# X^T of batches 2 to 7 by DMA transposes instead of TensorE transposes, with one more slot before the first use

## The chip, the cores and the metric

The kernel runs on one core of a Trainium2 chip. The metric is the device time of one execution in microseconds (us). Some executions are slower whatever the kernel; a run counts as slow here when it is over 1.5% above the fastest of the same kernel. Ratios and intervals use fast runs alone.

## The reference

Causal block attention over 8 batches, 8 heads, 576 positions and 64 dimensions per head, followed by a gated feed-forward block (FFN) with an RMS norm in front. Cut to what matters:

```python
scores = where(block_i >= block_j, (q @ k.T) / sqrt(64), -1e9)     # blocks of 64
x   = (softmax(scores) @ v)            # to [4608 tokens, 512]
xn  = x / sqrt(mean(x*x) + 1e-6) * rms_g
g   = xn @ w_gate                      # 512 -> 1536
out = (g * sigmoid(g) * (xn @ w_val)) @ w_out
```

The FFN needs `xn` transposed (d_model on the partitions); this is the X^T of the title.

## The kernel before

The kernel is a software pipeline of slots. A slot holds the attention of one pair of heads (four slots per batch) with pieces of FFN work from a queue placed between the parts of the attention. The FFN works on chunks of 512 tokens (the first two have 256). A chunk first runs 12 pairs of a gate and a value piece (four TensorE matmuls of 512 columns each), and then four rows of a down projection (twelve matmuls each). I call these its gate/value phase and its down phase. In the queue's units a chunk is 144, of which the first 96 are the gate/value phase.

Matmul results land in buffers of PSUM; a buffer can be taken for the next result once the one in it has been read for the last time. A plain copy out of PSUM is called an eviction here. The parts that the change touches (cuts are marked with `# ...`):

```python
def norm_scale(b, tiles):
    XN = xn_tiles[b]
    XS = xs.tile([P, n, DM], BF16, name="XS")
    # ... root(): 1/sqrt of the mean square, 13 small VectorE operations
    def one(j, t):
        rs = norm_tiles[b, tiles[0], "rs"]
        nc.vector.tensor_scalar(out=XS[:, j, :], in0=XN[:, t, :],
                                scalar1=rs[:, j:j + 1], scalar2=None, op0=ALU.mult)
    return [root] + [lambda j=j, t=t: one(j, t) for j, t in enumerate(tiles)]

def norm_transpose(b, tiles, p):          # p: one of four groups of 128 columns
    x = pf.tile([P, 2 * BANK], BF16, name="fps")           # PSUM
    for j in range(len(tiles)):
        pe(nc.tensor.transpose(x[:, j * P:(j + 1) * P], XS[:, j, p * P:(p + 1) * P], ident))
    # ... for each chunk touched: ScalarE copies x to XT, times gscale (rms_g)

def up_gate(i, m):
    pg = pf.tile([P, BANK], FP32, name="fps")              # pf: four PSUM buffers
    # ... four matmuls into pg; ScalarE: th = tanh(pg / 2); VectorE: th = (th + 1) * pg
def up_val(i, m):
    pv = pf.tile([P, BANK], FP32, name="fps")
    # ... four matmuls into pv; VectorE: HT = th * pv

def down(i, s, part):
    # ... twelve matmuls into one PSUM buffer po, in three parts
    if part == 2:
        ob = obuf.tile([P, DM], FP32, name="ob")           # obuf: two buffers
        nc.scalar.mul(out=ob, in_=po, mul=0.5)
        sp(nc.sync.dma_start(out=out[r0:r0 + P, :], in_=ob))   # SyncE's queue, kept in order

def ffn(cost):
    # ... while the budget lasts: the next piece of the queue, and after it
    #     one waiting piece of norm work: if aside: aside.pop(0)()
```

and the order of events for a batch (s0 is the slot after its last attention pair), with the end of each slot:

```python
    at(norms, s0, norm_squares)            # ScalarE
    at(norms, s0 + 1, norm_scale)          # VectorE
    s1 = s0 + 2
    at(norms, s1, xt_by_pe)                # TensorE transposes, ScalarE evictions
    at(rels, s1, release)                  # the chunk enters the queue at this slot's end
    ready.append(s1 + 1)
    # ... at the end of every slot, what the FFN pieces have not taken is run at once:
    for f in todo + aside + rels.pop(s, []) + pp + loads.pop(s, []):
        f()
```

The norm pieces of a slot start halfway through it. SyncE's queue carries three things in one order: the attention's own DMA transposes (QKT from QKN, 128x1920), the output stores, and, after the change, the new transposes.

The softmax here doesn't subtract the row's maximum and nothing guards it: scores larger than these inputs give would overflow.

## Time and profile before

| | before |
|---|---|
| time, median of the first three runs | 416.3 us (415.96 to 418.01) |
| TensorE busy | 376.6 us, 90% |
| VectorE, ScalarE busy | 61%, 59% |
| chain of waits | 74% TensorE, 11% ScalarE, 9% VectorE |
| TensorE transposes of XS | 160 |

The groups that the change touches (line, engine, operation, out<-in, shapes, count | busy us, mean ns of one | idle before, releaser), from the view that keeps shapes apart:

```profile
L342 DVE TENSOR_SCALAR XS<-XN,y 128x512 bf16<-128x512 f32 x40 | 20.2, 546 | 0.2
L355 PE MATMUL fps<-ident,XS 128*128 128x128 bf16 x160 | 14.9, 220 | 2.6 <-DVE XS L342 2.6
```

What VectorE does in the first of these stretches, in order of time (start us, length us):

```profile
135.95 0.49 DVE L342 TENSOR_SCALAR XS<-XN,y 128x512 bf16<-128x512 f32 x1
136.35 0.68 DVE L391 SCALAR_TENSOR_TENSOR th<-th,fps 128x512 f32<-128x512 f32 x1
136.95 0.64 DVE L342 TENSOR_SCALAR XS<-XN,y 128x512 bf16<-128x512 f32 x1
137.51 0.67 DVE L403 TENSOR_TENSOR HT<-th,fps 128x512 bf16<-128x512 f32 x1
138.10 1.40 DVE L342 TENSOR_SCALAR XS<-XN,y 128x512 bf16<-128x512 f32 x3
```

The last of the chunk's gate and value results (`th`, `HT`) stand among the first two scalings. The other three come after them, in the down phase, where VectorE has little to do (2.22 us busy from 140 to 150 us). TensorE waited for VectorE's `th` or `HT` for only 0.4 us in the whole span:

```profile
PE st L89 <- ACT PT_95 L260: 6.9, 7, 1.6
...
PE st L89 <- ACT PT_96 L260: 4.2, 6, 1.6
...
PE fps L89 <- DVE HT L403: 0.2, 1, 0.2
PE fps L89 <- DVE th L391: 0.2, 1, 0.2
```

(That view lists who waited for whom: us in total, times, longest.)

### The profile page before, as it was taken

What the parts mean: (1) busy time and instruction counts of PE and PEld (TensorE: products, weight loads), DVE (VectorE), ACT (ScalarE), POOL (GpSimd) and SP (SyncE); (2) the same over time, 40 slices, a digit from 0 to 9 for tenths busy, and PEclk for the clock granted to TensorE, in tenths of its full rate; (3) what the DMA queues carried; (4) which work ended last, traced back from release to release, by engine and by line L of the source; (5) the groups of instructions that cost most, each with busy time, mean ns of one, the idle gap of its engine ahead of it and who ended that gap; (6) DMA issues with size and microseconds to landing.
All of it is one profiled execution on the core that took longest, in us unless ns stands there. A gap on an engine that the chain in (4) does not pass through costs nothing.

```text
span 416.1 us, 7914 instructions
## 1 busy us (share of the span) xinstructions
PE 376.6 (90%) x2952; PEld 211.5 (51%) x3000; DVE 254.3 (61%) x698; ACT 245.6 (59%) x490; POOL 143.3 (34%) x200
## 2 busy tenths in 40 slices
PE   1367887988999999999999999999999999999996
PEld 0235764666555555555555555555555545444442
DVE  3554976669468546864785478447845881761760
ACT  2367877786767566756676667666765526322321
POOL 5532899987625903670349042000000000000000
PEclk9999999999999999999999999999999999999999
DMA  8999999999949975995699579342211002002002
GB/s 198 171 244 239 175 78 104 153 171 144 169 61 121 166 119 66 125 176 100 74 109 171 112 75 114 90 99 57 38 52 52 2 26 76 2 0 101 2 0 101
DMA packets 156277, 42.98 MB, mean 103 GB/s; under 512 B 142928, under 2 KB 151632, under 8 KB 156240
## 3 DMA queue, kind: packets, MB, share of 16 engines
q0 software_dynamic: 100512, 16.53, 54.0%
q1 hardware_dynamic: 55728, 25.96, 29.1%
q8 instruction: 23, 0.38, 0.4%
q14 instruction: 14, 0.11, 0.1%
HBM read 37.75 MB, written 9.44 MB: 113 GB/s over the span
## 4 chain that ended last, share of the span: by engine, by line
PE 74%; ACT 11%; DVE 9%; DMA 4%; issue 2%; SPq 0%; ACTq 0%; DVEq 0%
PE fps L89 57%; PE st L89 9%; PE X L89 6%; DMA HT<-in_k_dram 4%; ACT PT_95 L260 3%; ACT sq L327 2%; DVE th L391 2%; DVE HT L403 2%; ACT PT_96 L260 2%; PE fps L355 2%; ACT XT L362 2%; DVE XS L342 1%; ACT th L390 1%; DVE QKT L181 1%; DVE XN L294 1%
## 5 line engine op out<-in xcount | busy, mean ns | idle before, releaser
L89 PE MATMUL fps<-XT,WG 128*128 128x512 bf16 (+1 forms) x466 | 112.0, 357 | 1.2 <-DVE th L391 0.2
L89 PE MATMUL fps<-XT,WV 128*128 128x512 bf16 (+1 forms) x467 | 111.3, 357 | 0.5
L390 ACT ACTIVATE th<-fps 128x512 f32<-128x512 f32 (+1 forms) x120 | 66.8, 556 | 69.2 <-PE fps L89 66.4
L391 DVE SCALAR_TENSOR_TENSOR th<-th,fps 128x512 f32<-128x512 f32 (+1 forms) x120 | 75.8, 632 | 44.7 <-ACT th L390 44.1
L89 PE MATMUL fps<-WO,HT 128*128 128x512 bf16 x412 | 101.7, 379 | 1.2 <-DVE HT L403 0.2
L403 DVE TENSOR_TENSOR HT<-th,fps 128x512 bf16<-128x512 f32 (+1 forms) x120 | 75.9, 633 | 8.9 <-DVE th L391 0.5
L89 PEld LDWEIGHTS <-WG 128*128 128x128 bf16 x480 | 43.3, 98 | 38.6 <-issue 0.7
L89 PEld LDWEIGHTS <-WV 128*128 128x128 bf16 x480 | 43.5, 98 | 38.0
L260 ACT ACTIVATE PT_95<-st 128x512 bf16<-128x512 f32 (+3 forms) x70 | 51.0, 759 | 19.1 <-PE st L89 18.9
L89 PEld LDWEIGHTS <-HT 128*128 128x128 bf16 x432 | 38.8, 98 | 39.3 <-DVE HT L403 0.7
L260 ACT ACTIVATE PT_96<-st 128x1024 bf16<-128x1024 f32 (+3 forms) x67 | 51.0, 786 | 5.2 <-PE st L89 4.9
L417 ACT ACTIVATE ob<-fps 128x512 f32<-128x512 f32 x36 | 21.6, 599 | 51.8 <-PE fps L89 36.9
L89 PE MATMUL st<-QKT 128*128 128x320 bf16 (+3 forms) x240 | 43.1, 294 | 2.5 <-ACT PT_96 L260 1.2
L89 PEld LDWEIGHTS <-QKT 128*128 128x128 bf16 x288 | 27.0, 98 | 26.1 <-issue 3.0
L80 POOL DMA_DIRECT2D VN_94<-in_v_dram x20 | 17.0, 865 | 48.5 <-PE X L89 35.3
L294 DVE TENSOR_TENSOR XN<-X,rd 128x320 f32<-128x320 f32 (+2 forms) x72 | 32.4, 453 | 1.7
L362 ACT ACTIVATE XT<-fps,gscale 128x256 bf16<-128x256 bf16 (+6 forms) x68 | 28.8, 501 | 3.4 <-PE fps L355 3.3
L80 POOL DMA_DIRECT2D VN_93<-in_v_dram x20 | 18.5, 959 | 31.0 <-PE X L89 30.6
L267 DVE MEMSET PT_96<- 64x64 uint32 (+2 forms) x64 | 6.9, 112 | 35.8 <-ACT PT_96 L260 32.8
L80 POOL DMA_DIRECT2D QKN_92<-in_k_dram x30 | 22.9, 762 | 10.7 <-issue 9.9
L327 ACT ACTIVATE sq<-XN 128x512 bf16<-128x512 f32 x40 | 25.3, 633 | 0.1
L80 POOL DMA_DIRECT2D QKN_91<-in_k_dram x30 | 22.7, 757 | 5.3 <-issue 3.4
(82 smaller groups left out, 334.5 us busy)
## 6 DMA issues: line engine op xcount, KB each, us to landing
out_dram<-ob SPq DMA_DIRECT2D x36, 256.0 KB, 2.0
VN_93<-in_v_dram POOLq DMA_DIRECT2D x16, 128.0 KB, 5.6
VN_94<-in_v_dram POOLq DMA_DIRECT2D x16, 128.0 KB, 6.4
WG<-in_moe_w_gate_dram POOLq DMA_DIRECT2D x4, 384.0 KB, 13.7
WV<-in_moe_w_val_dram POOLq DMA_DIRECT2D x4, 384.0 KB, 16.5
WO<-in_moe_w_out_dram POOLq DMA_DIRECT2D x2, 768.0 KB, 25.7
QKN_91<-in_k_dram POOLq DMA_DIRECT2D x24, 64.0 KB, 4.0
QKN_91<-in_q_dram POOLq DMA_DIRECT2D x24, 64.0 KB, 3.8
```

What stands on the lines that cost most here:

```text
L80: return chain("POOL", nc.gpsimd.dma_start(**kw))
L89: pe(nc.tensor.matmul(dst, w, r, start=start, stop=stop))
L260: nc.scalar.activation(out=self.PT[:, n * T4 + a:n * T4 + e], in_=st[:, a:e], func=AF.Exp, scale=SM_SCALE)
L267: nc.vector.memset(blk[:, :, 0:BLK], 0.0)
L294: nc.vector.tensor_tensor(out=xn_tiles[self.b][:, t0:t0 + n, hd * D:(hd + 1) * D], in0=xv[:, :, 0:D], in1=rd.to_broadcast([P, n, D]), op=A ...
L327: nc.scalar.activation(out=sq, in_=XN[:, t, :], func=AF.Square, accum_out=ss[:, j:j + 1])
L355: pe(nc.tensor.transpose(x[:, j * P:(j + 1) * P], XS[:, j, p * P:(p + 1) * P], ident))
L362: nc.scalar.activation(out=xt_tiles[i][:, p, lo - a:hi - a], in_=x[:, lo - g0:hi - g0], func=AF.Copy, scale=gscale[:, p:p + 1])
L390: nc.scalar.activation(out=th[:, 0:n], in_=pg[:, 0:n], func=AF.Tanh, scale=0.5)
L391: nc.vector.scalar_tensor_tensor(out=th[:, 0:n], in0=th[:, 0:n], scalar=1.0, in1=pg[:, 0:n], op0=ALU.add, op1=ALU.mult)
L403: nc.vector.tensor_tensor(out=ht_tiles[i][:, m, :], in0=th[:, 0:n], in1=pv[:, 0:n], op=ALU.mult)
L417: nc.scalar.mul(out=ob, in_=po, mul=0.5)
```

## The change

The intent is to take the transposes of XS off the busiest engine. For batches 2 to 7 the XS tile is transposed by DMA from SyncE's queue straight into XT. The ScalarE copy that applied rms_g goes with the TensorE transposes, so the scaling takes rms_g, broadcast over the partitions in GB, as a second operand. The chunk's release is put one slot later, so that the transposes have time to land.

```diff
+    GB = const.tile([P, DM], FP32, name="GB")
@@ norm_scale
         def one(j, t):
             rs = norm_tiles[b, tiles[0], "rs"]
-            nc.vector.tensor_scalar(out=XS[:, j, :], in0=XN[:, t, :],
-                                    scalar1=rs[:, j:j + 1], scalar2=None, op0=ALU.mult)
+            if b >= 2:
+                nc.vector.scalar_tensor_tensor(out=XS[:, j, :], in0=XN[:, t, :],
+                                               scalar=rs[:, j:j + 1], in1=GB,
+                                               op0=ALU.mult, op1=ALU.mult)
+                turn(b, t, XS[:, j, :])
+            else:
+                # ... as before
+
+    def turn(b, t, src):
+        # ... for each chunk that the tile touches:
+                sp(nc.sync.dma_start_transpose(out=xt_tiles[i][:, :, lo - a:hi - a],
+                                               in_=src[lo - g0:hi - g0, :]))
@@ start
+    nc.sync.dma_start(out=GB, in_=moe_rms_g.partition_broadcast(P))
@@ order of events
-        at(norms, s1, lambda b=b, tiles=tiles: xt_by_pe(b, tiles))
+        if not b >= 2:
+            at(norms, s1, lambda b=b, tiles=tiles: xt_by_pe(b, tiles))
+        else:
+            s1 += 2 - 1
```

More of the change, by code (lines that the diff above doesn't have):

```diff
@@ L341, in one @@
             rs = norm_tiles[b, tiles[0], "rs"]
-            nc.vector.tensor_scalar(out=XS[:, j, :], in0=XN[:, t, :],
-                                    scalar1=rs[:, j:j + 1], scalar2=None, op0=ALU.mult)
-        return [root] + [lambda j=j, t=t: one(j, t) for j, t in enumerate(tiles)]
+            if b >= 2:
[4 more added lines that the diff above has]
+            else:
+                nc.vector.tensor_scalar(out=XS[:, j, :], in0=XN[:, t, :],
+                                        scalar1=rs[:, j:j + 1], scalar2=None, op0=ALU.mult)
+        return [root] + [lambda j=j, t=t: one(j, t) for j, t in enumerate(tiles)]
+    def turn(b, t, src):
+        g0 = b * S + t * P
+        g1 = min(g0 + P, (b + 1) * S)
+        for i, (a, e) in enumerate(chunks):
+            lo, hi = max(a, g0), min(e, g1)
+            if lo < hi:
+                if i not in xt_tiles:
+                    xt_tiles[i] = xtp.tile([P, HP, e - a], BF16, name="XT")
+                sp(nc.sync.dma_start_transpose(out=xt_tiles[i][:, :, lo - a:hi - a],
+                                               in_=src[lo - g0:hi - g0, :]))
     bounds = [0, 256] + list(range(512, NT + 1, 512))
```

## The prediction

> **What bounds the kernel.** TensorE. In stretches of 10 us, TensorE is 97 to 100% busy from 110 us to 410 us; the chain of waits is 74% TensorE. Busy time hides small gaps, so I summed issue spacings from the timeline: a feed-forward (FFN) matmul of 512 columns takes 0.2155 us (four in 0.862 us), the attention of one head pair about 2.26 us, a group of five TensorE transposes 0.28 us (142.23 to 142.51 us). From 108 us to the end that is 1164 x 0.2155 + 21 x 2.26 + 24 x 0.28 = 305 us for 303.5 us of time. No hidden stall is left to recover; time falls only by TensorE work removed after 108 us. Before 108 us TensorE is 70 to 90% busy.
>
> **What the change removes.** 120 of the 160 transposes, in 24 groups, all after 108 us: 24 x 0.28 = 6.7 us of TensorE, all on the critical path. Also 48 of the 68 ScalarE evictions into X^T (about 0.5 us each) and 24 PSUM tiles; off the path. The page's 14.9 us of transpose busy time (11.2 us for 120) overstates it: neighbours overlap part.
>
> **What it adds.** 30 VectorE scalings with a second operand instead of a plain scalar: 0.48 us each now, estimated 0.55 to 0.69 us (this operation reading PSUM takes 0.686 us). At most 6 us on an engine 61% busy: off the path. 33 DMA transposes of up to 128x512 on SyncE's queue. The existing transposes, 3.75 times larger, hold the queue for 1.4 to 3.6 us and land 4.1 to 9.4 us (median 5.1) after issue; scaled, about 0.5 us of issue each. The Trainium skill's "DMA: Bandwidth & Descriptors" (Latency and other measured facts) gives 261 GB/s effective with a non-contiguous middle dimension; this trace's transposes with their fixed time come to less than 100 GB/s, and I use the trace. The last piece is issued about the end of its slot; the first use comes a full slot (about 9.8 us) plus the 12-unit reserve (2.6 us) later, so it should land in time. The scale row adds 256 KB at the start, when DMA is full: 0 to 1 us.
>
> **What it moves.** FFN chunks of batches 2 on are released one slot later. Steady slots keep their FFN share, but slots 11 to 15 spread one chunk's 132 units over five slots instead of four: 26 units, about 8 us instead of 9.8 us per slot. In the thinner slots before (83 to 97 us) TensorE lost 0.3 to 0.9 us at a time to exponentials queued behind squares. I expect 0 to 1.5 us lost there, mostly in slot 12, which has the squares. The displaced work runs later, where TensorE is dense.
>
> **Sum.** -6.7, +0.7 (thin slots), +0.4 (start): 416.3 - 5.6 = 410.7 us. Range 408.8 to 413.5. Faster by over 2% (below 408.0) 0.07, within 2% 0.89, slower 0.04.
>
> **What would show it.** TensorE transposes 40 instead of 160, X^T evictions 20; TensorE busy about 11 us less; still 98% or more from 150 us to the end; no TensorE wait on a DMA transpose; small new waits on exponentials between 108 and 150 us; first dense moment within 1 us of before.
>
> **What would make it wrong.** Transposes landing late (SyncE's in-order queue, or slow 64-row pieces), which would show as TensorE waiting for the DMA at a chunk's first gate matmul. Loads slowed by DMA contention, stalling attention. Thin slots losing far more than 1.5 us.

## More of the kernel before

The busy shares of the whole span average over stages. The page's 40 slices (10.4 us each, busy tenths) show them apart. TensorE is the limit from about slice 11 on; before that it is not full.

```profile
span 416.1 us, 7914 instructions
...
PE 376.6 (90%) x2952; PEld 211.5 (51%) x3000; DVE 254.3 (61%) x698; ACT 245.6 (59%) x490; POOL 143.3 (34%) x200
...
PE   1367887988999999999999999999999999999996
DVE  3554976669468546864785478447845881761760
```

Windows of 10 us (start:end, length, then busy us of TensorE, its weight loads, VectorE, ScalarE and GpSimd with instruction counts, granted clock, DMA share, GB/s). These are the stretches that the argument comes back to:

```profile
130.00:140.00 10.00, 9.89 (x77) 5.29 (x78) 9.41 (x31) 5.21 (x9) 5.93 (x9) 1.00 1.44 126
170.00:180.00 10.00, 9.95 (x77) 5.28 (x78) 9.48 (x31) 5.44 (x10) 6.62 (x11) 1.00 1.40 125
330.00:340.00 10.00, 9.95 (x47) 4.57 (x47) 8.79 (x25) 5.36 (x13) 0.00 (x0) 1.00 0.01 2
```

TensorE is full, but look at the third number: VectorE is busy 8.8 to 9.5 us of these 10. That engine is at 61% over the whole span and at 88 to 95% in one stretch per batch.

## The result and the profile after

The changed kernel took 421.87 us in the median of 4 runs (421.27 to 422.69), the kernel before in the same rounds 416.5 us (415.96 to 418.01). Its result is right. The ratio is 1.0124, with a 95% interval of 1.0093 to 1.0156. A ratio here is the mean time of one kernel's fast runs over that of the other's of the same rounds, so it is not quite the ratio of the medians that I quote. I had predicted 410.7 us, in a range of 408.8 to 413.5.

```profile
span 420.9 us, 7762 instructions
...
PE 375.1 (89%) x2880; PEld 205.2 (49%) x2880; DVE 256.8 (61%) x698; ACT 228.5 (54%) x442; POOL 142.3 (34%) x200
...
PE   1458787988999999899989998999899989999996
DVE  3555975667479637952795379537953881761760
```

TensorE's row now has an 8 in five places, one for each of batches 3 to 7. (The totals of TensorE's busy time cannot be compared: the trace of before lacks some matmul records, for instance 20 of the 432 down-projection matmuls.) The groups:

```profile
L344 DVE SCALAR_TENSOR_TENSOR XS<-XN,y,GB 128x512 bf16<-128x512 f32 x30 | 20.9, 748 | 0.1
...
L373 PE MATMUL fps<-ident,XS 128*128 128x128 bf16 x40 | 4.5, 233 | 2.4 <-DVE XS L349 2.4
```

The transposes are gone as planned, 160 to 40. The scaling of batches 2 to 7 takes 748 ns; the median of the old one is 483 ns. The windows of the same places:

```profile
130.00:140.00 10.00, 8.63 (x75) 4.62 (x73) 9.14 (x25) 5.30 (x9) 9.84 (x15) 1.00 1.53 110
170.00:180.00 10.00, 8.53 (x71) 4.47 (x69) 9.70 (x23) 4.53 (x7) 8.77 (x12) 1.00 2.08 115
330.00:340.00 10.00, 8.31 (x38) 3.49 (x36) 9.73 (x26) 2.99 (x6) 0.00 (x0) 1.00 0.09 15
```

TensorE lost about 1.5 us in each, while VectorE was at 9.1 to 9.7 of 10. One of these places, first VectorE's order and then TensorE's:

```profile
170.96 0.69 DVE L421 TENSOR_TENSOR HT<-th,fps 128x512 bf16<-128x512 f32 x1
...
171.76 1.41 DVE L344 SCALAR_TENSOR_TENSOR XS<-XN,y,GB 128x512 bf16<-128x512 f32 x2
173.09 0.68 DVE L409 SCALAR_TENSOR_TENSOR th<-th,fps 128x512 f32<-128x512 f32 x1
173.69 2.07 DVE L344 SCALAR_TENSOR_TENSOR XS<-XN,y,GB 128x512 bf16<-128x512 f32 x3
...
175.97 0.69 DVE L421 TENSOR_TENSOR HT<-th,fps 128x512 bf16<-128x512 f32 x1
```

```profile
170.74 1.03 PE L89 MATMUL fps<-XT,WV 128*128 128x512 bf16 x4
171.60 1.03 PE L89 MATMUL fps<-XT,WG 128*128 128x512 bf16 x4
...
172.92 1.03 PE L89 MATMUL fps<-XT,WV 128*128 128x512 bf16 x4
...
174.22 1.03 PE L89 MATMUL fps<-XT,WG 128*128 128x512 bf16 x4
176.71 1.02 PE L89 MATMUL fps<-XT,WV 128*128 128x512 bf16 x4 [1.47 <-DVE HT L421]
```

The value result of 170.74 us lies in PSUM until VectorE does its `HT` at 175.97 us, because all five scalings stand in front of it: two before the `th` that this `HT` needs, and three after it. The four PSUM buffers then hold the results of 170.74, 171.60, 172.92 and 174.22 us, and TensorE cannot start the next value piece until that `HT` frees the oldest. (That the buffers are full is read from this order; no run changed their number.) The waits of TensorE in the whole span:

```profile
PE fps L89 <- DVE HT L421: 7.5, 5, 1.6
PE st L89 <- ACT PT_95 L261: 6.9, 7, 1.6
PE st L89 <- ACT PT_96 L261: 4.9, 7, 1.6
...
PE fps L89 <- DVE th L409: 2.3, 4, 1.4
```

The waits for `HT` and `th` are 9.8 us against 0.4 us before; those for the exponentials (`PT`) are 11.8 us against 11.1 us. No TensorE wait on a DMA is listed. The shown wait is a little short, because the ends of matmuls are modelled: from start to start, the next value piece was due 0.86 us after 174.22 us, at 175.08 us, and came at 176.71 us, 1.63 us late where the view says 1.47. With 0.16 us more for each of the six long waits, the sum is 9.4 + 1.0 + 0.7 = 11.1 us given back against 6.7 us removed, 4.4 us slower; the spans of the two profiles differ by 4.8 us.

### The profile page after: what moved, and what is told of

It is laid out like the page before. It is cut to its first block, busy times and chain, and to the rows that moved or that the text cites. A ratio compares the mean times of both kernels' runs of the same rounds, so it can differ in the third digit from the quotient of the medians.

```text
span 420.9 us, 7762 instructions
## 1 busy us (share of the span) xinstructions
PE 375.1 (89%) x2880; PEld 205.2 (49%) x2880; DVE 256.8 (61%) x698; ACT 228.5 (54%) x442; POOL 142.3 (34%) x200
## 4 chain that ended last, share of the span: by engine, by line
PE 49%; DVE 23%; ACT 17%; issue 6%; DMA 3%; SPq 0%; DVEq 0%; ACTq 0%
PE fps L89 40%; PE st L89 6%; DVE th L409 5%; DVE HT L421 5%; ACT sq L328 5%; ACT PT_95 L261 4%; DVE XS L344 4%; DMA HT<-in_k_dram 3%; PE X L89 3%; ACT PT_96 L261 2%; ACT th L408 2%; DVE XN L295 2%; ACT XT L380 2%; DVE XS L349 1%; DVE QKT L182 1%
## 5 line engine op out<-in xcount | busy, mean ns | idle before, releaser
L89 PE MATMUL fps<-XT,WV 128*128 128x512 bf16 (+1 forms) x480 | 112.9, 358 | 7.5 <-DVE HT L421 7.5
L89 PE MATMUL fps<-XT,WG 128*128 128x512 bf16 (+1 forms) x480 | 113.2, 358 | 2.7 <-DVE th L409 2.3
L294 DVE RECIPROCAL rd<-X 128x5 f32<-128x5 f32 (+2 forms) x72 | 13.2, 186 | 21.6 <-PE X L89 21.0
L268 DVE MEMSET PT_96<- 64x64 uint32 (+2 forms) x64 | 6.9, 112 | 31.8 <-ACT PT_96 L261 29.7
L80 POOL DMA_DIRECT2D QKN_92<-in_k_dram x30 | 23.4, 781 | 6.7 <-DMA QKT<-QKN_92 6.3
L268 DVE MEMSET PT_95<- 64x64 uint32 (+2 forms) x64 | 6.6, 112 | 31.2 <-ACT PT_95 L261 29.4
```

The source lines that it names most:

```text
L80: return chain("POOL", nc.gpsimd.dma_start(**kw))
L89: pe(nc.tensor.matmul(dst, w, r, start=start, stop=stop))
L268: nc.vector.memset(blk[:, :, 0:BLK], 0.0)
L294: nc.vector.reciprocal(out=rd, in_=xv[:, :, D:D + 1])
```

## The experiments

The theories at the start were these. PLACE: the extra slot moved the scalings from the start of the down phase into the gate/value phase. (The traces show them at 63 to 77% of its length in batches 3 to 6.) LENGTH: the scaling takes longer. DMA: the transposes disturb the rest by contention. As three things changed together, I ran their combinations. In the labels, `p` has TensorE transposes and `d` DMA transposes; `shift` has the extra slot; `long` has the two-operand scaling.

| run | median us | before, same rounds | ratio (95% interval) | right result |
|---|---|---|---|---|
| after (`d`, shift, long) | 421.87 | 416.5 | 1.0124 (1.0093 to 1.0156) | yes |
| d_noshift_long | 432.56 | 418.46 | 1.0337 (1.0247 to 1.0426) | yes |
| d_noshift_short | 432.63 | 418.46 | 1.0339 (1.0251 to 1.0427) | no |
| d_shift_short | 416.97 | 418.46 | 0.998 (0.9915 to 1.0046) | no |
| p_shift_long | 428.96 | 418.46 | 1.0268 (1.0204 to 1.0333) | yes |
| p_shift_short | 425.94 | 416.77 | 1.0197 (1.0165 to 1.0229) | yes |
| p_noshift_long | 418.1 | 416.77 | 1.0016 (0.9987 to 1.0045) | yes |
| d_shift_long_spread2 | 412.65 | 416.77 | 0.9898 (0.9865 to 0.9932) | yes |
| d_noshift_long_ob4 | 411.26 | 416.77 | 0.9853 (0.9826 to 0.988) | yes |
| d_noshift_long_ob3 | 412.69 | 417.02 | 0.9882 (0.9843 to 0.9921) | yes |
| d_noshift_long_actout | 411.68 | 417.02 | 0.986 (0.9826 to 0.9895) | yes |
| d_shift_long_ob4 | 420.72 | 417.02 | 1.0082 (1.0043 to 1.0121) | yes |
| d_b1_noshift_ob4 | 412.35 | 417.02 | 0.9883 (0.9844 to 0.9923) | yes |

The medians of the rounds with 418.46 us contain one slow run of the kernel before and one of d_noshift_long; the ratios leave them out.

### 1. No DMA transposes, but the extra slot and the long scaling

```diff
+        if b >= 2:
+            s1 += 1          # xt_by_pe stays at s0 + 2, release moves
         at(rels, s1, ...)
```
and the scaling with GB, the ScalarE eviction with scale 1.0 for batches 2 to 7.

> The kernel before with TensorE transposes kept, but with the extra slot and the two-operand scaling (right result). PLACE, LENGTH and both-needed: the same VectorE waits without any new DMA, so 416.4 + 9 to 10 = 425 to 427 us. DMA: within 1.5 us of the kernel before, 416 to 418 us.

Measured: ratio 1.0268. That is about 11 us more than before, where PLACE expected 9 to 10. TensorE's waits for `HT` and `th` are 7.4 and 2.6 us, nearly the same as in the changed kernel, without one new DMA of XS. The theory DMA is out as the cause of the loss. Beside it, the changed kernel (1.0124) differs only in the path of the transpose, and its profiled span is 6.6 us shorter (427.5 to 420.9). So the transposes by DMA brought about the predicted 6.7 us (the ratios, from different rounds, give 6 us with about 3 us either way); what came with them cost more.

### 2. The parts alone with TensorE transposes

> The kernel before with the two-operand scaling and the scale row's load alone (TensorE transposes, no extra slot; right result). The scalings fall at the end of the gate/value phase, where VectorE has time: ratio 1.000 to 1.004. If length is all: ratio 1.015 or more. A cost of the scale row at the start would show here too.

Measured: ratio 1.0016. The longer scaling in its old place costs nothing clear of noise, and neither does the row's load at the start. VectorE is busy 9.36 to 9.55 us of 10 in the stretches from 130, 170 and 210 us of this trace, and TensorE 10.00: a nearly full VectorE alone does no harm.

> The kernel before with the extra slot alone (TensorE transposes, old scaling; right result). If place and length both count, as the wrong-result run with the short scaling suggests (4.5 us of waits left, 7.4 and 2.6 us with the long one): about 4 to 5 us more than before, ratio 1.009 to 1.013. If place is all: ratio 1.024 or more. If place is nothing: 1.00.

Measured: ratio 1.0197, more than I had expected for this case and less than PLACE alone asked for. The waits for `HT` and `th` shown are 2.4 and 2.7 us, so the shown waits explain only some 5 us of the 8. The rest is in what the view leaves out. Measured from start to start, less the usual spacing of the same two pieces, TensorE lost 8.0 us after 108 us in this trace and 1.0 us in that of p_noshift_long; the two spans differ by 7.8 us. The extra slot is a cost by itself, with the old scaling and the old transposes.

### 3. The changed kernel with the short scaling

```diff
-                nc.vector.scalar_tensor_tensor(out=XS[:, j, :], ..., in1=GB, ...)
+                nc.vector.tensor_scalar(out=XS[:, j, :], ..., scalar2=None, op0=ALU.mult)
```

> The changed kernel with the old one-operand scaling, so the scale row is left out for batches 2 to 7: wrong result on purpose. PLACE alone: about 420 us, the waits of TensorE on VectorE stay near 1.4 us each. LENGTH: the waits shrink by 5 x 0.22 = 1.1 us to about 0.4 us each, 414 to 415 us. If both are needed: 414 to 415 us here and 410 to 412 us without the extra slot. DMA: about 421 us.

Measured: 0.998, 416.97 us, between what LENGTH and what PLACE expected. The waits for `HT` and `th` fall from 9.8 to 4.5 us, but they do not go. The 1.4 points between this run and the changed kernel are the price of the two-operand scaling there; the intervals are 0.3 to 0.65 points either way. They understate the price of length, because the old scaling was not always short in this run: 10 of its 30 took 0.60 to 0.82 us, all in batches 2 to 4. Batch by batch (the five scalings together, and what TensorE lost around them from start to start, both in us, worked out from the traces):

| batch | d_shift_short: scalings, lost | changed kernel: scalings, lost |
|---|---|---|
| 2 | 3.89, 1.71 | 3.74, 1.54 |
| 3 | 2.79, 0.70 | 3.73, 1.63 |
| 4 | 2.96, 0.88 | 3.74, 1.64 |
| 5 | 2.42, 0.30 | 3.74, 1.64 |
| 6 | 2.41, 0.30 | 3.75, 1.63 |
| 7 | 2.42, 0.92 | 3.73, 2.28 |

In p_noshift_long the scalings take 3.7 us in every batch too, and TensorE loses less than 0.1 us around them in each of batches 2 to 6 and 0.9 us in batch 7. So both are needed: the place makes the wait possible, and its size follows how long the five scalings take. (Every one-operand scaling over 0.49 us in this trace and in those of the kernel before and of p_shift_short ran beside a busy GpSimd, and every one with GpSimd idle took 0.47 to 0.49 us. No run tested whether GpSimd is the cause.)

### 4. The changed kernel without the extra slot

```diff
-            s1 += 2 - 1
+            pass
```

> The changed kernel without the extra slot; DMA transposes and the two-operand scaling stay. Theory PLACE (the extra slot moves the five scalings of a batch from the end of a chunk's gate/value phase into its middle, where VectorE must free PSUM for TensorE): the six waits of about 1.5 us go, 410 to 412 us. Theory LENGTH (the scaling is simply longer, five times about 0.22 us more in a row): still about 420 us. Theory DMA (queue or memory contention from the transposes): about 420 us or more, and with less slack the transposes may be late at a chunk's first gate matmul.

> DMA transposes alone: no extra slot, old scaling (wrong result on purpose). PLACE, LENGTH and both-needed all expect what I predicted for the whole change, 409.5 to 411.5 us, that is the 6.7 us of TensorE transposes gone and nothing given back. DMA: 418 us or more.

Measured: 1.0337 and 1.0339. PLACE and LENGTH missed. DMA had said "about 420 us or more" and had named contention on the queue; these runs do not contradict it, though it is out as the cause of the changed kernel's loss. The waits on VectorE did go, as PLACE said (0.8 and 0.2 us left), but another wait took their place, and a larger one:

```profile
ACT ob L435 <- DMA out_dram<-ob: 27.0, 5, 6.6
...
PE st L89 <- ACT PT L261: 21.6, 16, 4.2
```

ScalarE waits for an output buffer, five times and up to 6.6 us. The exponentials stand behind it in ScalarE's order, and TensorE behind the exponentials. SyncE's queue (start us, us from the first issue to the last, count) shows why, and TensorE's timeline what follows:

```profile
135.76 5.33 SPq L361 DMA_TRANSPOSE XT<-XS  x4
141.44 3.36 SPq L210 DMA_TRANSPOSE QKT<-QKN  x1
144.90 5.49 SPq L437 DMA_DIRECT2D out_dram<-ob  x3
```

```profile
150.99 1.01 PE L89 MATMUL st<-QKT 128*128 128x512 bf16 x3 [4.18 <-ACT PT L261]
151.81 1.90 PE L89 MATMUL fps<-XT,WG 128*128 128x512 bf16 x4
153.50 1.91 PE L89 MATMUL fps<-XT,WV 128*128 128x512 bf16 x4
```

A new transpose holds SyncE's queue for 1.2 us (median 1216 ns) and the attention's one for 3.4 us here. So the queue was taken from 134.5 us (this view cuts off the first of the five transposes) until 144.9 us. Output rows were ready meanwhile, with two buffers to hold them. Without the extra slot this falls into the down phase, which is when the stores are due. After the wait of 4.18 us TensorE also ran at half speed: the matmuls start 1.69 us apart per group of four (151.81 to 153.50) instead of 0.86. The Trainium skill's "TensorE: Matmul & The Clock Gate" (What's actually happening) says that the clock falls to half after an idle window of about 3.4 us. This trace agrees: the mean granted clock is 0.68 from 150 to 160 us, and its record in the trace is 0.5 from 149.5 to 156.3 us. After the waits of 1.5 us in the changed kernel it stayed at 1.00.

The new theory, QUEUE, which makes the queue part of DMA precise: the order on SyncE's queue makes the stores late. It was tested in three ways.

### 5. More output buffers, and another queue for the stores

```diff
-    obuf = ctx.enter_context(tc.tile_pool(name="obuf", bufs=2))
+    obuf = ctx.enter_context(tc.tile_pool(name="obuf", bufs=4))    # or 3
```

> DMA transposes and two-operand scaling without the extra slot, and four output buffers instead of two. Theory QUEUE (without the extra slot the transposes, 1.2 us of SyncE's queue each, stand ahead of the output stores; ScalarE then waits for an output buffer, 6.4 us at the longest, and the exponentials behind it hold TensorE about 4 us per batch): with four buffers a whole chunk's rows fit, the waits go, and the time is the kernel before less 5.5 to 6.7 us, ratio 0.984 to 0.988. Rival LATE (X^T itself arrives late) or CLOCK (transposes lower the granted clock by themselves): stays near ratio 1.03.

Measured: ratio 0.9853, 411.26 us. No wait of ScalarE for an output store is listed any more (two of 0.6 us in front of `ob` are put down to a new transpose). The windows of the worst stretches, first with two buffers, then with four:

```profile
140.00:150.00 10.00, 6.76 (x49) 3.45 (x48) 0.37 (x3) 2.36 (x5) 2.52 (x4) 0.97 1.93 173
150.00:160.00 10.00, 8.85 (x47) 4.33 (x48) 4.53 (x12) 5.16 (x9) 0.00 (x0) 0.68 0.40 102
```

```profile
140.00:150.00 10.00, 10.00 (x79) 5.29 (x78) 2.79 (x12) 4.77 (x8) 4.25 (x6) 1.00 2.10 160
150.00:160.00 10.00, 10.00 (x80) 5.28 (x78) 7.65 (x17) 5.76 (x10) 0.00 (x0) 1.00 0.82 194
```

TensorE went from 6.76 to 10.00 us of 10, with the same transposes in the same stretch and the clock back at 1.00. The rivals LATE and CLOCK are out.

> Dose: three output buffers, no extra slot. SyncE's queue is held for about 10 us by five or six transposes and one of the attention's; output rows come every 3.5 us there, so three buffers bridge most of it: store waits of ScalarE fall from 24 us to under 8 us, ratio 0.985 to 1.005. If the store wait is not the cause: 1.03 as with two.

Measured: 0.9882; ScalarE's store waits are 13.3 us, more than the 8 us that I had allowed, but at 3.8 us the longest is short enough that TensorE's waits for exponentials (11.2 us) are as before. The time is as expected.

```diff
-            sp(nc.sync.dma_start(out=out[r0:r0 + P, :], in_=ob))
+            nc.scalar.dma_start(out=out[r0:r0 + P, :], in_=ob)     # two buffers
```

> DMA transposes and two-operand scaling, no extra slot, two output buffers as before, but the output stores are issued from ScalarE's queue, so that they cannot stand behind the transposes on SyncE's queue. QUEUE (order on SyncE's queue is the cause): as good as four output buffers, ratio to before 0.984 to 0.992, no wait of ScalarE for an output buffer over 1 us. If the stores are slow because the DMA engines themselves are taken by the transposes: ScalarE still waits several us per batch, ratio over 1.01.

Measured: 0.986. The time is as QUEUE expects. A detail was not: ScalarE still waited 9.5 us in all and 3.6 us at the longest, and a store's median landing grew from 2.0 to 3.1 us, so the stores do share something with the transposes; it does not reach TensorE (11.5 us of waits for exponentials). The Trainium skill's "DMA: Bandwidth & Descriptors" (Issuing engines are not separate DMA queues) says that starting DMAs on several engines saves only the sequencer's time, "which is usually small relative to the DMA itself". This case is one where it is not small: 1.2 us of issue for a transpose that lands after 3.9 us (median, changed kernel), in one queue with stores that are needed; moving the stores took the ratio from 1.0337 to 0.986, about 20 us.

> Control: the changed kernel (extra slot kept) with four output buffers. The buffers cure only the store wait, which the extra slot already avoids, so nothing changes: ratio to before 1.009 to 1.016, waits of TensorE on VectorE still 9 to 10 us. If the buffers were a gain by themselves: under 1.00.

Measured: 1.0082, slightly under the range expected, and the waits for `HT` and `th` are 7.4 and 2.0 us. Four buffers are no gain by themselves; they cure only what removing the slot brings up.

### 6. The extra slot kept, the scalings spread

```diff
+            odd[0] += 1
-            if aside:
+            if aside and (odd[0] % 2 or not spread[0]):
                 aside.pop(0)()
@@ end of slot
+        carry = s in scales                 # slots with scalings of batches 2 to 7
-        for f in todo + aside + ...
+        for f in todo + ([] if carry else aside) + ...
```

> The changed kernel with the extra slot, but the five scalings of a batch are handed out one per two feed-forward pieces, also across the end of the slot, instead of the rest in one block at the slot's end. BLOCK (it is the block of scalings in the middle of the gate/value phase that holds PSUM): the waits of TensorE on VectorE, 9.8 us in the changed kernel, fall under 2 us, ratio to before 0.984 to 0.992. LENGTH alone (VectorE simply has too much work in that slot): waits stay above 6 us, ratio 1.00 or more.

Measured: 0.9898, and the waits for `HT` and `th` are 0.2 us. All 30 long scalings are still there; they only no longer stand in a block. Of the 30, 24 still start in the gate/value phase; the other six, each the last or the last two of its batch, start in the down phase. VectorE's order in one batch, and the window in which the changed kernel's TensorE had 8.53 us:

```profile
212.32 0.75 DVE L344 SCALAR_TENSOR_TENSOR XS<-XN,y,GB 128x512 bf16<-128x512 f32 x1
212.99 0.68 DVE L411 SCALAR_TENSOR_TENSOR th<-th,fps 128x512 f32<-128x512 f32 x1
...
213.88 0.69 DVE L423 TENSOR_TENSOR HT<-th,fps 128x512 bf16<-128x512 f32 x1
214.49 0.75 DVE L344 SCALAR_TENSOR_TENSOR XS<-XN,y,GB 128x512 bf16<-128x512 f32 x1
```

```profile
170.00:180.00 10.00, 10.00 (x80) 5.29 (x78) 9.62 (x23) 5.43 (x9) 8.89 (x12) 1.00 1.41 117
```

VectorE is as full as in the changed kernel (9.62 against 9.70 us), and TensorE is full too (10.00). This settles the mechanism for the changed kernel: it is the block of scalings in front of `HT`, not the amount of VectorE work in the stretch and not the extra slot as a delay.

### 7. Batch 1 too

```diff
-            if b >= 2:      # scaling and turn
+            if b >= 1:
-        if not b >= 2:      # xt_by_pe
+        if not b >= 1:
```
on top of four buffers and no extra slot.

> Candidate for the best: four output buffers, no extra slot, and batch 1 also by DMA transposes. Batch 1's four groups of transposes are 4 x 0.28 = 1.1 us and TensorE waited 1.2 us for its scalings; so 1 to 3 us below the version with batches 2 to 7, ratio 0.978 to 0.984. If the earlier batch is hurt by the loads of that time (DMA is busiest before 110 us): 0.985 or more.

Measured: 0.9883, a miss: no better than without it (0.9853, in other rounds). In place of the waits for batch 1's scalings TensorE waits once, at 102.76 us, for 2.21 us, for VectorE's `XN`. I did not follow this further.

## Why the prediction was wrong

- **What bounds the kernel, and the 6.7 us of TensorE work: right.** The pair p_shift_long and changed kernel differ by 6.6 us of span, and d_noshift_long_ob4 comes out 1.5% below before, about 6.1 us.
- **"off the path" for the 30 scalings ("At most 6 us on an engine 61% busy"): this is the step that failed, together with the next.** I judged VectorE by its share of the whole span. In the 10 us of a batch where the scalings run it was already 88 to 95% busy before. That alone does no harm (p_noshift_long, the spread scalings); the step failed because the scalings came to stand in a block in front of the `HT` that frees PSUM. What it measured: 9.8 us of TensorE waits on VectorE (0.4 before) where the sum has nothing. The length was also a little under-estimated (0.748 us against 0.55 to 0.69). In the old place the length is harmless (1.0016); in the new one it is more than half of the loss (1.64 us a batch with long scalings, 0.30 in the two steady batches where all five were short).
- **"What it moves": wrong about what moves.** I followed the FFN units per slot, found that "Steady slots keep their FFN share", and expected 0 to 1.5 us lost in slots 11 to 15. But the extra slot also moves the chunk's phases against the norm work, which stays where it was. Before, a chunk starts in slot s0 + 3 of its batch, and the next batch's scalings, at s0 + 5, fall at two thirds of it, the end of the gate/value phase. After, it starts at s0 + 4 and the same scalings fall inside the gate/value phase, with about a quarter of it still to come. The loss is in every batch, in steady slots and in the tail. The thin slots themselves lost about what I had allowed: from 108 to 130 us TensorE lost 1.6 us from start to start, 1.08 of it at 108.2 us, where exponentials stand behind six X^T evictions of batch 1 on ScalarE, and not behind the squares that I had named.
- **Start: right.** The first scores of batch 2 are at 82.95 us against 83.30 us before.
- **The transposes land in time: right.** No TensorE wait on a DMA is listed. But the issue was mis-sized: 1.2 us each where I scaled to "about 0.5 us". That did no harm in the changed kernel, because the extra slot keeps the transposes out of the down phase; without the slot it cost more than everything else here.
- **The signs I named:** 40 transposes and 20 evictions, right; "98% or more from 150 us to the end", wrong (85% at 170 to 180 us), and this is the sign that showed the failure; TensorE's total busy time was no usable sign because of missing records.

The prediction's list of what could go wrong had late transposes, contention and the thin slots. It did not have the cause.

What stays open: why the DMA path gained a little more between the two short-scaling kernels (1.0197 to 0.998) than between the two long ones (1.0268 to 1.0124), which the intervals nearly allow; whether the busy GpSimd is what lengthens the one-operand scaling; and how many PSUM buffers would have hidden the block.

## What to carry to other kernels

Before calling added work "off the path", look at the engine in the stretch where the work will stand and at what its queue frees next: five short operations in a block in front of the one that frees PSUM stop a TensorE that an even spread of the same operations does not. A change of when work is released moves it against everything that stays, so redraw which phases meet, not only how much each slot holds. And count the issue time on an in-order DMA queue as occupancy: what stands behind it needs buffers for as long as the queue is held, or another queue. Here the intended gain was had nearly in full (about 6.1 of 6.7 us) with two edits, no extra slot and two more output buffers: 411.26 us against 416.77 us.

## What the Trainium skill lacked or had wrong

- "DMA: Bandwidth & Descriptors", Issuing engines are not separate DMA queues: calls the issue time usually small. Here a DMA transpose of up to 128x512 in SBUF held SyncE's queue for 1.18 to 2.02 us (median 1.22) and landed after a median of 3.9 us, and moving 36 stores to another engine's queue was worth about 20 us (ratio 1.0337 to 0.986).
- The same page, Latency and other measured facts: 261 GB/s for DMA transposes is no guide to when a small one lands. 128 KB in 3.9 us from issue to landing is 34 GB/s; the 480 KB ones, at 5.1 us, came to 96 GB/s. Issued back to back, one per 1.22 us, the small ones come to about 107 GB/s (an estimate from these figures).
- "VectorE: DVE Perf Modes", The perf-mode tier table: this table has no row for `scalar_tensor_tensor` (other pages of the skill have general notes on such operations). With two f32 operands in SBUF it took 748 ns for 512 elements, and `tensor_scalar` 483 ns in the median (up to 825); the table's two tiers for `tensor_scalar` and `tensor_tensor` point the same way.
- "TensorE: Matmul & The Clock Gate", What's actually happening: nothing wrong. A wait of 4.18 us came with 6.8 us at half speed, and waits of 1.5 us brought none.
